# SwiGLU feed-forward on one core: the first half block of x by a crossbar copy instead of TensorE transposes, with a new order of loads and matmuls in the head

## Chip, core and metric

The kernel runs on one NeuronCore of one Trainium2 chip. The metric is the device time in microseconds (us) of that core. Three runs of the kernel before gave 163.2, 163.65 and 164.01 us, median 163.65 us.

## The reference

All tensors are bf16. B = 1, S = 2048 rows, D = 640, F = 1536.

```
g = silu(x @ w_gate)      # x [1, 2048, 640], w_gate [640, 1536]
u = x @ w_up              # w_up [640, 1536]
return (g * u) @ w_down   # w_down [1536, 640]
```

## The kernel before

The matmuls contract over the partitions, so x is needed transposed: `xT` holds 5 slices (`kd`) of 128 values of D on the partitions, and all 2048 rows of x along the free axis. S is cut into 4 blocks (`sb`) of 512 rows, F into 12 chunks (`fc`) of 128. For each block and chunk, five matmuls over `kd` make the gate `pg` and five make the up projection `pu`, both [128, 512] in PSUM; `gate` (L210) applies Silu on ScalarE and multiplies on VectorE, which writes the chunk to `aT`. After the 12 chunks of a block follow the down projection into `po_t` (the last 128 columns of D, transposed) and `po_a` (the first 512), and the output is sent off. VectorE also works out the last four rows of the output's hidden layer by dot products (`row_dots`), beside TensorE.

The part at issue is the start, `head` (L219). There the first block's first four chunks (`EARLY` = 4) are treated apart, since nothing has been loaded yet:

- TensorE runs 18 matmuls on a tile of ones (`warm`, L174), whose result is not used.
- Rows 0 to 255 of x are loaded as they lie (`load_x`, L85: one DMA of 128 rows on SyncE's queue, one on ScalarE's), and transposed by TensorE: `transpose_chunk` (L180), twice five transposes into PSUM, which ScalarE and VectorE copy to `xT`. This needs the identity matrix `ident`, made on GpSimd.
- Rows 256 to 511 are transposed on the way from memory by `turn_x` (L104), a crossbar copy (`dma_start_transpose`) on SyncE's queue. The later blocks' x comes in the same way.
- The order of the gate's matmuls is written out in `steps` (L230 to 235): for each `kd` the four chunks on rows 0 to 255, then for each `kd` the four chunks on rows 256 to 511; 44 matmuls in all. Then, chunk by chunk, the up projection on all 512 rows (20 matmuls of 512 columns) and the gate's Silu and product.

SyncE issues its DMAs in the order of the program (`keep_order`, L315). In the head it is: x rows 0 to 127, `w_gate` of the four early chunks in four DMAs by `kd` (the fifth, `kd` 1, on ScalarE's queue, L114), the crossbar copy of rows 256 to 511 (L118), `w_up` of the four early chunks in two DMAs (L121), then `w_gate` and `w_up` of chunks 4 to 7 and of chunks 8 to 11 (L123, L124), `w_down` (L125), and the crossbar copy of the second block's rows (L135). TensorE and ScalarE also run in the order of the program. The early loads are of these sizes: x rows 0 to 255 and 256 to 511, 320 KB each; `w_gate` and `w_up` of four chunks, 640 KB each.

Of the kernel before, what the change touches and what calls it, by code (L numbers as in the profile page):

```python
# [7 lines left out]


@with_exitstack  # L10
def _body(
# [8 lines left out]
    nc = tc.nc  # L20
    P = nc.NUM_PARTITIONS
    f32 = mybir.dt.float32
    bf16 = mybir.dt.bfloat16
# [3 lines left out]
    B, S0, D = x.shape  # L27
    F = w_gate.shape[1]
    S = B * S0
    x2 = x.rearrange("b s d -> (b s) d")  # L30
    out2 = out.rearrange("b s d -> (b s) d")

    KD = D // P
    KF = F // P
    S_BLK = 512
    NSB = S // S_BLK
    SUB = S_BLK // P
    HALF = S_BLK // 2
    DA = 512
    Q = 32  # L40
    N_WARM = 18
    T = 4
    WT_STEP = 4
    ROW_J = 0
    EARLY = 4
# [3 lines left out]
    consts = ctx.enter_context(tc.tile_pool(name="consts", bufs=1))  # L49
    work = ctx.enter_context(tc.tile_pool(name="work", bufs=3))  # L50
    outp = ctx.enter_context(tc.tile_pool(name="outp", bufs=3))
    psum = ctx.enter_context(
        tc.tile_pool(name="psum", bufs=2, space=bass.MemoryType.PSUM)
    )

    ident = consts.tile([P, P], bf16)
    x_sb = consts.tile([P, HALF // P, D], bf16)
    xT = consts.tile([P, KD, S], bf16)
    wg_sb = consts.tile([P, KD, F], bf16)
    wu_sb = consts.tile([P, KD, F], bf16)  # L60
# [7 lines left out]
    row_s = consts.tile([P, KF, T], f32)  # L68
    prod = consts.tile([P, D], f32)

    make_identity(nc, ident[:])

    x_v = x2.rearrange("(c p) d -> p c d", p=P)
    xt_v = x2.rearrange("s (kd p) -> s kd p", p=P)
    wg_v = w_gate.rearrange("(kd p) f -> p kd f", p=P)
    wu_v = w_up.rearrange("(kd p) f -> p kd f", p=P)
# [2 lines left out]
    def wslice(a, b):  # L79
        return slice(a * P, b * P)  # L80

    def load_w(eng, dst, src, a, b):
        eng.dma_start(out=dst[:, :, wslice(a, b)], in_=src[:, :, wslice(a, b)])

    def load_x(eng, c0, c1):  # L85
        eng.dma_start(out=x_sb[:, c0:c1, :], in_=x_v[:, c0:c1, :])  # L86

    def issue_order(a, b):
        tc.add_manual_dep(
# [8 lines left out]
    def keep_order(engine):  # L98

        traced = [i for i in nc.cur_bb.bb.instructions if i.engine == engine]  # L100
        for a, b in zip(traced, traced[1:]):
            issue_order(a, b)

    def turn_x(r0, r1):  # L104
        nc.sync.dma_start_transpose(out=xT[:, :, r0:r1], in_=xt_v[r0:r1])
# [2 lines left out]
    silu_first = consts.tile([P, 1], f32)  # L108
    nc.vector.memset(ones[:], 1.0)  # L109

    load_x(nc.sync, 0, 1)
    load_x(nc.scalar, 1, 2)
    for kd in range(KD):
        eng = nc.scalar if kd == 1 else nc.sync  # L114
        eng.dma_start(
            out=wg_sb[:, kd, wslice(0, EARLY)], in_=wg_v[:, kd, wslice(0, EARLY)]
        )
    turn_x(HALF, S_BLK)  # L118
    nc.scalar.activation(silu_first[:], ones[:, 0:1], ACT.Silu)  # L119
    for a in range(0, EARLY, 2):  # L120
        load_w(nc.sync, wu_sb, wu_v, a, a + 2)  # L121
    for a, b in W_CHUNKS:
        load_w(nc.sync, wg_sb, wg_v, a, b)  # L123
        load_w(nc.sync, wu_sb, wu_v, a, b)  # L124
# [4 lines left out]
    def turn_w(dst, src, f0, f1):  # L129
# [7 lines left out]
        out=x_row[:],  # L137
        in_=x2[S - T : S, :].rearrange("t d -> (t d)").partition_broadcast(P),
# [35 lines left out]
    def warm(n):  # L174
        for _ in range(n):
            nc.tensor.matmul(  # L176
                pw[:, 0:P], lhsT=ones[:], rhs=ones[:], start=True, stop=True
            )

    def transpose_chunk(c, parts):  # L180
        c_sl = slice(c * P, (c + 1) * P)
        for copy, tag, k0, k1 in parts:
            pt = psum.tile([P, k1 - k0, P], bf16, tag=tag, name="pt")
            for kd in range(k0, k1):
                nc.tensor.transpose(  # L185
                    out=pt[:, kd - k0, :],
                    in_=x_sb[:, c, kd * P : (kd + 1) * P],
                    identity=ident[:],
                )
            copy(out=xT[:, k0:k1, c_sl], in_=pt[:])  # L190

    def proj_step(ps, w_sb, fc, sb, c0, c1, kd):
        nc.tensor.matmul(  # L193
            ps[:, c0:c1],
            lhsT=w_sb[:, kd, fc * P : (fc + 1) * P],
            rhs=xT[:, kd, sb * S_BLK + c0 : sb * S_BLK + c1],
            start=(kd == 0 and c0 in (0, HALF)),
            stop=(kd == KD - 1),
        )

    def proj(ps, w_sb, fc, sb, c0, c1):
        for kd in range(KD):
            proj_step(ps, w_sb, fc, sb, c0, c1, kd)

    def gu_tiles():
        pg = psum.tile([P, S_BLK], f32, tag="gu", name="pg", bufs=4)
        pu = psum.tile([P, S_BLK], f32, tag="gu", name="pu", bufs=4)
        return pg, pu

    def gate(pg, pu, sb, fc, n_s):  # L210

        s0 = sb * S_BLK
        sg = work.tile([P, S_BLK], f32, name="sg")
        nc.scalar.activation(sg[:, 0:n_s], pg[:, 0:n_s], ACT.Silu)  # L214
        nc.vector.tensor_tensor(  # L215
            out=aT[:, fc, s0 : s0 + n_s], in0=sg[:, 0:n_s], in1=pu[:, 0:n_s], op=ALU.mult
        )

    def head():  # L219
        dve, act = nc.vector.tensor_copy, nc.scalar.copy  # L220
        split = [(act, "po_a", 0, 2), (dve, "po_b", 2, KD)]
        pgs = [
            psum.tile([P, S_BLK], f32, tag="gu", name="pg", bufs=4)
            for _ in range(EARLY)
        ]
        warm(N_WARM)
        for c in range(HALF // P):
            transpose_chunk(c, split)

        steps = [(0, 0, P), (0, P, HALF)]  # L230
        steps += [(kd, 0, HALF) for kd in range(1, KD)]
        steps += [(kd, HALF, S_BLK) for kd in range(KD)]
        for kd, c0, c1 in steps:
            for fc in range(EARLY):
                proj_step(pgs[fc], wg_sb, fc, 0, c0, c1, kd)

        for fc in range(EARLY):
            pu = psum.tile([P, S_BLK], f32, tag=("po_a", "po_b")[fc % 2], name="pu")
            proj(pu, wu_sb, fc, 0, 0, S_BLK)
            gate(pgs[fc], pu, 0, fc, S_BLK)  # L240
        keep_order(mybir.EngineType.PE)
        keep_order(mybir.EngineType.Activation)

    head()
    for sb in range(NSB):
        n_s = S_BLK if sb < NSB - 1 else S_BLK - T
        for fc in range(KF):
            if sb == 0 and fc < EARLY:
                continue
            pg, pu = gu_tiles()  # L250
# [22 lines left out]
        for q in range(P // Q):  # L273
            nc.scalar.dma_start(
                out=out2[
                    sb * S_BLK : sb * S_BLK + n_t, DA + q * Q : DA + (q + 1) * Q
                ].rearrange("(i r) c -> r i c", r=Q),
                in_=ot_q[q * Q : (q + 1) * Q, :].rearrange("r (i c) -> r i c", c=Q),
            )

        for j in range(SUB):
# [6 lines left out]
            for c0, c1, tag in cols:  # L288
# [14 lines left out]
                eng = nc.sync if c1 < D else nc.scalar  # L303
# [82 lines left out]
def kernel(tc, *args):  # L386
    _body(tc, *args)
    tc.close()
    tc.compile()
    _trim(tc.nc)  # L390
# [30 lines left out]
```

## Time and profile before

| | |
|---|---|
| three runs | 163.2, 163.65, 164.01 us |
| span of the profiled execution, first to last instruction | 161.8 us |
| time of the runs less that span | 1.4, 1.85 (median) and 2.2 us |
| granted TensorE clock, as the page has it | 1.00 |
| TensorE busy | 159.4 us, 99% of the span |
| VectorE, ScalarE, GpSimd busy | 111.0, 42.6, 0.6 us |
| read from memory, written to it | 6.88 MB, 2.62 MB |

The profiled execution's own time outside of its span isn't given; which of the three runs is nearest to it can't be told. "PE" is TensorE's matmuls, "PEld" its loads of weights, "DVE" VectorE, "ACT" ScalarE, "SPq" the issuing of DMAs by SyncE. A matmul's duration holds the time that it takes to drain, so the rate is read from how many begin in a stretch, not from the mean duration. In the list of DMA issues the last number is the time from issue to landing.

### The profile page before, as it was taken

The numbers are of one execution on the slowest core, as the hardware profiler recorded it, in microseconds if no ns is written. First come the engines' busy times: TensorE is split into PE (matmuls) and PEld (weight loads), VectorE is DVE, ScalarE is ACT, GpSimd is POOL, SyncE is SP. The second block draws the span as 40 slices with busy tenths as digits, with TensorE's granted clock in tenths as the row PEclk, the third lists the DMA queues.
The fourth block names the chain that finished last, engine by engine and source line by source line (L and its number), as shares of the span: only waits on it lengthen the run. The fifth ranks groups of instructions, "written<-read, shape, count | busy, mean of one in ns | idle before, by whom it ended". The sixth has DMA issues, their size and how long they took to land.

```text
span 161.8 us, 2142 instructions
## 1 busy us (share of the span) xinstructions
PE 159.4 (99%) x808; PEld 77.6 (48%) x808; DVE 111.0 (69%) x250; ACT 42.6 (26%) x74; POOL 0.6 (0%) x6
## 2 busy tenths in 40 slices
PE   8999999999999999999999999999999999999995
PEld 7854444444444444444444444444444444445454
DVE  2034223599569999989919999979964999993001
ACT  5051222112222222211222322221214222222121
POOL 1000000000000000000000000000000000000000
PEclk9999999999999999999999999999999999999999
DMA  6999999934189999003110000000321000000312
GB/s 212 231 351 349 361 248 231 222 75 91 34 192 159 235 236 184 4 0 34 65 65 0 0 4 2 0 0 3 62 67 34 0 0 0 0 0 4 48 41 73
DMA packets 41961, 15.86 MB, mean 98 GB/s; under 512 B 33504, under 2 KB 41824, under 8 KB 41952
## 3 DMA queue, kind: packets, MB, share of 16 engines
q1 hardware_dynamic: 33584, 14.93, 37.0%
q10 hardware_dynamic: 8368, 0.80, 3.5%
q8 instruction: 6, 0.10, 0.3%
q14 instruction: 3, 0.02, 0.1%
HBM read 6.88 MB, written 2.62 MB: 59 GB/s over the span
## 4 chain that ended last, share of the span: by engine, by line
PE 97%; DMA 2%; SPq 0%; DVE 0%; issue 0%
PE pg L193 32%; PE pu L193 32%; PE po_a L291 26%; PE po_t L261 6%; DMA wg_sb<-in_w_gate_dram 2%; SPq L86 0%; DVE ot_b L302 0%
## 5 line engine op out<-in xcount | busy, mean ns | idle before, releaser
L193 PE MATMUL pg<-xT,wg_sb 128*128 128x512 bf16 (+3 forms) x264 | 59.8, 363 | 0.1
L193 PE MATMUL pu<-xT,wu_sb 128*128 128x512 bf16 (+1 forms) x240 | 59.1, 379 | 0.0
L215 DVE TENSOR_TENSOR aT<-sg,pu 128x512 bf16<-128x512 f32 (+1 forms) x48 | 32.7, 682 | 32.3 <-PE pu L193 32.3
L214 ACT ACTIVATE sg<-pg 128x512 f32<-128x512 f32 (+1 forms) x48 | 28.4, 597 | 71.2 <-PE pg L193 67.4
L291 PE MATMUL po_a<-wd_sb,aT 128*128 128x512 bf16 (+4 forms) x228 | 42.8, 348 | 0.0
L147 DVE SCALAR_TENSOR_TENSOR prod<-wgT,x_row 128x640 f32<-128x640 bf16 x48 | 39.4, 821 | 1.5 <-DMA wgT<-in_w_gate_dram 0.4
L147 DVE SCALAR_TENSOR_TENSOR prod<-wuT,x_row 128x640 f32<-128x640 bf16 x48 | 39.4, 821 | 1.0
L193 PEld LDWEIGHTS <-wg_sb 128*128 128x128 bf16 x264 | 25.9, 100 | 26.8 <-DMA wg_sb<-in_w_gate_dram 0.4
L193 PEld LDWEIGHTS <-wu_sb 128*128 128x128 bf16 x240 | 23.4, 98 | 28.1 <-DMA wu_sb<-in_w_up_dram 0.3
L291 PEld LDWEIGHTS <-aT 128*128 128x128 bf16 x228 | 20.8, 98 | 21.7
L300 ACT CAST ot<-po_a 128x512 bf16<-128x512 f32 (+2 forms) x17 | 9.5, 559 | 31.8 <-PE po_a L291 20.2
L261 PE MATMUL po_t<-aT,wd_sb 128*128 128x512 bf16 (+1 forms) x48 | 10.4, 366 | 0.0
L261 PEld LDWEIGHTS <-wd_sb 128*128 128x128 bf16 x48 | 4.7, 98 | 5.1
L302 DVE CAST ot_b<-po_a 128x96 bf16<-128x96 f32 (+1 forms) x2 | 0.5, 240 | 9.7 <-PE po_a L291 9.6
L270 ACT CAST ot_t<-po_t 128x512 bf16<-128x512 f32 (+1 forms) x4 | 2.2, 559 | 11.6 <-PE po_t L261 11.6
L147 DVE DVE_READ_ACCUMULATOR prod<-wgT,x_row 128x1 f32 x48 | 3.9, 82 | 0.0
L147 DVE DVE_READ_ACCUMULATOR prod<-wuT,x_row 128x1 f32 x48 | 3.9, 82 | 0.0
L272 DVE STREAM_TRANSPOSE ot_q<-ot_t 128x512 bf16<-128x512 bf16 (+1 forms) x4 | 2.7, 676 | 1.7 <-ACT ot_t L270 1.7
L190 DVE COPY xT<-pt 128x384 bf16<-128x384 bf16 x2 | 0.7, 358 | 2.9 <-PE pt L185 2.9
L176 PE MATMUL pw<-ones 128*128 128x128 bf16 x18 | 2.1, 313 | 0.4 <-DVE ones L109 0.4
L176 PEld LDWEIGHTS <-ones 128*128 128x128 bf16 x18 | 1.8, 147 | 0.4 <-DVE ones L109 0.4
L119 ACT ACT_TABLE_LOAD x1 | 1.3, 1283 | 1.0 <-issue 1.0
(13 smaller groups left out, 4.7 us busy)
## 6 DMA issues: line engine op xcount, KB each, us to landing
wd_sb<-in_w_down_dram SPq DMA_DIRECT2D x1, 1920.0 KB, 13.0
out_dram<-ot SPq DMA_DIRECT2D x15, 128.0 KB, 1.7
wg_sb<-in_w_gate_dram SPq DMA_DIRECT2D x2, 640.0 KB, 7.9
wu_sb<-in_w_up_dram SPq DMA_DIRECT2D x2, 640.0 KB, 8.6
wu_sb<-in_w_up_dram SPq DMA_DIRECT2D x2, 320.0 KB, 4.7
x_row<-in_x_dram SPq DMA_DIRECT2D x1, 640.0 KB, 5.1
wg_sb<-in_w_gate_dram SPq DMA_DIRECT2D x4, 128.0 KB, 3.4
out_dram<-ot_q ACTq DMA_DIRECT2D x12, 32.0 KB, 1.9
```

Of the source, the lines that this page charges most:

```text
L119: nc.scalar.activation(silu_first[:], ones[:, 0:1], ACT.Silu)
L147: nc.vector.scalar_tensor_tensor(out=prod[:], in0=wT[:, fc, :], scalar=1.0, in1=x_row[:, t, :], op0=ALU.mult, op1=ALU.mult, accum_out=acc[ ...
L176: nc.tensor.matmul(pw[:, 0:P], lhsT=ones[:], rhs=ones[:], start=True, stop=True)
L190: copy(out=xT[:, k0:k1, c_sl], in_=pt[:])
L193: nc.tensor.matmul(ps[:, c0:c1], lhsT=w_sb[:, kd, fc * P : (fc + 1) * P], rhs=xT[:, kd, sb * S_BLK + c0 : sb * S_BLK + c1], start=(kd == 0 ...
L214: nc.scalar.activation(sg[:, 0:n_s], pg[:, 0:n_s], ACT.Silu)
L215: nc.vector.tensor_tensor(out=aT[:, fc, s0 : s0 + n_s], in0=sg[:, 0:n_s], in1=pu[:, 0:n_s], op=ALU.mult)
L261: nc.tensor.matmul(po_t[:], lhsT=wd_sb[:, kf, DA:D], rhs=aT[:, kf, sb * S_BLK : sb * S_BLK + n_t], start=(kf == 0), stop=(kf == KF - 1),)
L270: nc.scalar.copy(ot_t[:], po_t[:])
L272: nc.vector.transpose(out=ot_q[:], in_=ot_t[:])
L291: nc.tensor.matmul(po[:], lhsT=aT[:, kf, s0 : s0 + P], rhs=wd_sb[:, kf, c0:c1], start=(kf == 0), stop=(kf == KF - 1),)
L300: nc.scalar.copy(ot[:], po[:])
```

## The change

Rows 0 to 255 of x now come by `turn_x`, as the first DMA on SyncE's queue; `ident`, `x_sb`, the ten TensorE transposes and their four copies are gone. All loads of the head are on SyncE's queue; `w_gate` of the early chunks comes in three DMAs (`kd` 0; 1 and 2; 3 and 4). The crossbar copy of rows 256 to 511 is issued behind both DMAs of `w_up` instead of before them. There are 26 warming matmuls instead of 18. TensorE's order in the head is: gate of the four chunks on rows 0 to 255 (20 matmuls of 256 columns, `kd` outermost), up of the four chunks on rows 0 to 255 (20), gate of the four chunks on rows 256 to 511 (20), up on rows 256 to 511 (20), each of the last four groups of five followed by `gate`. The up projections take all four PSUM buffers of `po_a` and `po_b` at once. Behind the head nothing is changed.

```diff
-    N_WARM = 18
+    N_WARM = 26
...
-    ident = consts.tile([P, P], bf16)
-    x_sb = consts.tile([P, HALF // P, D], bf16)
...
-    make_identity(nc, ident[:])
...
-    load_x(nc.sync, 0, 1)
-    load_x(nc.scalar, 1, 2)
-    for kd in range(KD):
-        eng = nc.scalar if kd == 1 else nc.sync
+    def load_d(eng, k0, k1):
         eng.dma_start(
-            out=wg_sb[:, kd, wslice(0, EARLY)], in_=wg_v[:, kd, wslice(0, EARLY)]
+            out=wg_sb[:, k0:k1, wslice(0, EARLY)], in_=wg_v[:, k0:k1, wslice(0, EARLY)]
         )
-    turn_x(HALF, S_BLK)
+
     nc.scalar.activation(silu_first[:], ones[:, 0:1], ACT.Silu)
+    turn_x(0, HALF)
+    load_d(nc.sync, 0, 1)
+    load_d(nc.sync, 1, 3)
+    load_d(nc.sync, 3, KD)
     for a in range(0, EARLY, 2):
         load_w(nc.sync, wu_sb, wu_v, a, a + 2)
+    turn_x(HALF, S_BLK)
...
         warm(N_WARM)
-        for c in range(HALF // P):
-            transpose_chunk(c, split)
-
-        steps = [(0, 0, P), (0, P, HALF)]
-        steps += [(kd, 0, HALF) for kd in range(1, KD)]
-        steps += [(kd, HALF, S_BLK) for kd in range(KD)]
+        steps = [(kd, 0, HALF) for kd in range(KD)]
         for kd, c0, c1 in steps:
             for fc in range(EARLY):
                 proj_step(pgs[fc], wg_sb, fc, 0, c0, c1, kd)
-
+        pus = [
+            psum.tile([P, S_BLK], f32, tag=("po_a", "po_b")[fc % 2], name="pu")
+            for fc in range(EARLY)
+        ]
         for fc in range(EARLY):
-            pu = psum.tile([P, S_BLK], f32, tag=("po_a", "po_b")[fc % 2], name="pu")
-            proj(pu, wu_sb, fc, 0, 0, S_BLK)
-            gate(pgs[fc], pu, 0, fc, S_BLK)
+            proj(pus[fc], wu_sb, fc, 0, 0, HALF)
+
+        for fc in range(EARLY):
+            proj(pgs[fc], wg_sb, fc, 0, HALF, S_BLK)
+        for fc in range(EARLY):
+            proj(pus[fc], wu_sb, fc, 0, HALF, S_BLK)
+            gate(pgs[fc], pus[fc], 0, fc, S_BLK)
```

More of the change, by code (lines that the diff above doesn't have):

```diff
@@ L6 @@
 from concourse._compat import with_exitstack
-from concourse.masks import make_identity
 @with_exitstack
@@ L69, in _body @@
     prod = consts.tile([P, D], f32)
-    make_identity(nc, ident[:])
-    x_v = x2.rearrange("(c p) d -> p c d", p=P)
     xt_v = x2.rearrange("s (kd p) -> s kd p", p=P)
@@ L83, in load_w @@
         eng.dma_start(out=dst[:, :, wslice(a, b)], in_=src[:, :, wslice(a, b)])
-    def load_x(eng, c0, c1):
-        eng.dma_start(out=x_sb[:, c0:c1, :], in_=x_v[:, c0:c1, :])
     def issue_order(a, b):
@@ L178, in warm @@
             )
[L180 to L190, printed above, removed]
     def proj_step(ps, w_sb, fc, sb, c0, c1, kd):
@@ L219, in head @@
     def head():
-        dve, act = nc.vector.tensor_copy, nc.scalar.copy
-        split = [(act, "po_a", 0, 2), (dve, "po_b", 2, KD)]
         pgs = [
```

## The prediction

> **What bounds the kernel now.** First the page: busy times, and the chain that ended last.
>
> ```profile
> PE 159.4 (99%) x808; PEld 77.6 (48%) x808; DVE 111.0 (69%) x250; ACT 42.6 (26%) x74; POOL 0.6 (0%) x6
> ...
> PE 97%; DMA 2%; SPq 0%; DVE 0%; issue 0%
> ...
> L176 PE MATMUL pw<-ones 128*128 128x128 bf16 x18 | 2.1, 313 | 0.4 <-DVE ones L109 0.4
> ```
>
> TensorE carries the whole span, so the time is: the moment at which it begins useful work, plus that work, plus holes. The change leaves the work as it is and touches only the start, so the second view is the chain of the first 16 us.
>
> ```profile
> 0.45 3.21 DMA wg_sb<-in_w_gate_dram
> 3.66 0.05 issue
> 3.71 5.21 PE pg L193 x44
> 8.92 4.37 PE pu L193 x20
> 13.29 1.08 PE pg L193 x5
> ```
>
> From 3.71 us on TensorE is on the chain without a break. The head is over when the first ordinary group begins: 13.12 us in the timeline of TensorE (the chain counts ends and says 13.29). From there groups of five take 1.08 us each to the end. Whatever moves 13.12 moves the time by as much.
>
> ```profile
> 0.39 2.10 PE L176 MATMUL pw<-ones 128*128 128x128 bf16 x18 [0.39 <-DVE ones L109]
> 2.31 1.25 PE L185 MATMUL pt<-ident,x_sb 128*128 128x128 bf16 x10
> ...
> 13.12 1.24 PE L193 MATMUL pg<-xT,wg_sb 128*128 128x512 bf16 x5
> 14.20 1.03 PE L193 MATMUL pu<-xT,wu_sb 128*128 128x512 bf16 x4
> ```
>
> Third, the rate, from the stretches' counts of matmuls (one that began earlier is counted too).
>
> ```profile
> 3.71:4.95 1.24, 1.24 (x10) 1.00 1.01 265
> 4.97:6.48 1.51, 1.51 (x15) 1.00 0.86 185
> 6.57:8.75 2.18, 2.18 (x21) 1.00 0.97 291
> 8.79:13.12 4.33, 4.33 (x22) 1.00 1.07 353
> ```
>
> The 20 gate matmuls of 256 columns in 6.57 to 8.75 take 109 ns each, the 20 up matmuls of 512 columns 216 ns. The 18 warming matmuls of 128 columns, begun within 2.10 us less the last one's own 0.31 us (313 ns, the page's L176), stand 105 ns apart: as long as 256 columns take later. So the array begins at half speed, although the clock column says 1.00 throughout. In 3.71 to 4.95 us ten matmuls begin, eight of 128 and two of 256 columns, which would take 6 × 0.109 = 0.65 us at full speed; half speed costs the head 0.6 us now, and ends at about 5 us.
>
> Fourth, the loads: SyncE's issues (start, duration), then times to landing, each asked for in a stretch that holds that issue alone.
>
> ```profile
> 1.85 0.43 SPq L115 DMA_DIRECT2D wg_sb<-in_w_gate_dram  x1
> 2.33 1.91 SPq L105 DMA_TRANSPOSE xT<-in_x_dram  x1
> 4.29 1.15 SPq L83 DMA_DIRECT2D wu_sb<-in_w_up_dram  x2
> 5.49 0.52 SPq L83 DMA_DIRECT2D wg_sb<-in_w_gate_dram  x1
> 6.06 0.92 SPq L83 DMA_DIRECT2D wu_sb<-in_w_up_dram  x1
> ```
>
> ```profile
> x_sb<-in_x_dram ACTq DMA_DIRECT2D x1, 160.0 KB, 2.6
> wg_sb<-in_w_gate_dram SPq DMA_DIRECT2D x1, 128.0 KB, 3.4
> xT<-in_x_dram SPq DMA_TRANSPOSE x1, 4.2
> wu_sb<-in_w_up_dram SPq DMA_DIRECT2D x1, 320.0 KB, 4.9
> wg_sb<-in_w_gate_dram SPq DMA_DIRECT2D x1, 640.0 KB, 6.6
> wu_sb<-in_w_up_dram SPq DMA_DIRECT2D x1, 640.0 KB, 8.0
> ```
>
> With the issue times: x rows 0 to 255 are in at 2.7 us (ScalarE's DMA, issued at 0.13), the last early gate slice at 5.25, the crossbar copy at 2.33 + 4.2 = 6.5, the second early up load at 4.93 + 4.9 = 9.8, then gate 4 to 7 at 12.1 and up 4 to 7 at 14.0. TensorE wants the last at 14.2: only 0.2 us to spare. The loads therefore run close beside TensorE, and their order matters.
>
> **The change part by part.** *Removed:* identity, ten transposes, four copies. The transposes run from 2.31 to 3.3 us, in time in which TensorE otherwise waits for `w_gate` (ready at 3.66), so they free nothing. Two DMAs on ScalarE's queue go to SyncE; an issue takes some 0.4 us and SyncE stays ahead of the data. *Added:* 8 warming matmuls. 26 times 105 ns from 0.39 us end at 3.1 us; they delay nothing unless data come before that. *The work itself:* 80 matmuls of 256 columns at 109 ns, 8.72 us, against 40 × 109 + 20 × 216 = 8.68 us now. Nothing gained.
>
> *The price is in the arrivals.* Now the crossbar copy is hidden behind gate work on rows that came as plain loads. In the changed kernel everything waits for a crossbar copy, and the 40 matmuls on rows 256 to 511 (4.36 us) wait for a second one that stands behind 320 + 640 + 640 KB. Today the head's last data, at 9.8, leave 3.3 us of work behind them; there 4.36 us remain. To break even the second copy must land by 13.12 − 4.36 = 8.76 us.
>
> When does it land? First copy: bounded below by 2.7 us (the same 320 KB as plain loads at the start) and above by 4.2 (this copy behind the gate loads). Two copies of twice the size with a freer queue:
>
> ```profile
> 44.58 2.73 SPq L105 DMA_TRANSPOSE xT<-in_x_dram  x1
> ...
> xT<-in_x_dram SPq DMA_TRANSPOSE x1, 5.4
> ```
>
> ```profile
> 44.57:45.66 1.09, 1.09 (x7) 0.49 (x5) 0.00 (x0) 0.60 (x1) 0.00 (x0) 1.00 0.37 120
> 45.66:46.90 1.24, 1.24 (x7) 0.59 (x6) 1.13 (x2) 0.12 (x1) 0.00 (x0) 1.00 0.77 141
> 46.90:48.40 1.50, 1.50 (x9) 0.68 (x7) 1.47 (x5) 0.47 (x1) 0.00 (x0) 1.00 1.27 286
> ```
>
> The last column is GB/s. For 1.1 us only output stores move, then the copy runs at half rate for over a microsecond, then at 286 GB/s. A start of 1.1 us, 320 KB at these rates (175 KB in 1.24 us, the rest at 286 GB/s in 0.53) and 0.7 us from the last data to landing (today's copy, whose stretches stand below: data to about 5.8, landed at 6.5) give 3.6 us. I take 3.6, nearer to this row than to the plain loads. The Trainium skill ("Advanced Engine Details and Errata", X-Bar Transpose (TRN2)) says that transposing DMAs are as fast as regular ones, at 350 to 400 GB/s expected. The traced 286 GB/s after a stretch at 141 is below that. By the page the first copy would land with the plain loads, at 2.7.
>
> Behind a crossbar copy the queue has a hole. Here the stretches around today's landing at 6.5:
>
> ```profile
> 5.25:5.80 0.55, 0.00 (x0) 1.00 1.27 287
> 6.00:6.50 0.50, 0.00 (x0) 1.00 0.39 79
> 6.50:7.00 0.50, 0.00 (x0) 1.00 0.67 183
> 7.00:9.00 2.00, 0.00 (x0) 1.00 1.04 321
> ```
>
> So 640 KB behind a copy landed 9.8 − 6.5 = 3.3 us after it; the next 640 KB took 12.1 − 9.8 = 2.3 us; and a 320 KB copy landed 6.5 − 5.25 = 1.25 us behind the load ahead of it. By these landings: 3.6, gate 6.9, up 9.2, second copy 10.5 us. By bytes alone: after 3.6 the remaining 1.27 MB at 321 GB/s are 4.0 us, the slow ramp 0.3, the copy's 0.33 MB at 287 GB/s 1.1, landing 0.5: 9.5 us. The first counts how long the slowest of the DMA engines trails, the second doesn't; I take 10.1.
>
> First-half work: `kd` 0 lands some 0.9 us behind the copy, at 4.5 (an estimate from 128 of the 640 KB and the hole). Gate waits on the loads to 6.9, the last 8 of it end at 7.8, the 20 up matmuls wait for 9.2 at most and end at 10.3 by landings, sooner by bytes. So both ends meet near 10.1; then 4.36 us give 14.5 against 13.12: +1.35 us.
>
> *What is late next:* up 4 to 7. It landed 14.0 − 9.8 = 4.2 us behind the early up loads; behind a copy that is 3.3 + 2.3 = 5.6, at 15.7, and TensorE wants it at 14.5 + 1.08 = 15.6. I add 0.15 us. The loads for chunks 8 to 11 are wanted 8 groups or 8.6 us later, while their 1.31 MB take 4.1 us at 321 GB/s; the next crossbar copy is wanted by the second block, at least 16 groups or 17 us later. The new waits on PSUM are covered: the fifth gate group takes the buffer of the first, whose Silu can run as soon as its five matmuls on rows 256 to 511 are done, 3.8 us earlier. The fourth Silu waits for the first product's buffer, but its PSUM is wanted 3 us after the head.
>
> **Sum:** +1.35 + 0.15 = +1.5 us on the span of 161.8; with the 1.85 us by which the median exceeds that span, 163.65 + 1.5 = 165.15 us.
>
> **Rivals.** *A: the copy is as quick as a plain load and the loads keep their rate.* First copy at 2.7, second by bytes 5.9 us later, at 8.6, below the 8.76 of the break-even. Then TensorE itself is the bound: from `kd` 0 at 3.5 us with 8.72 us of work and some 0.7 us lost to half speed, the head ends at 12.9: −0.2 us, 163.45, not slower. For it speaks the 287 GB/s that a copy reaches; against it the first microsecond without data and the hole, which both stand in rows. It decides from a second landing before 8.8; in between lie times within 0.5%.
>
> *B: the array stays at half speed.* Between the warming's end at 3.1 and `kd` 0 at 4.5 TensorE is idle for 1.4 us, against 0.4 today, and then it waits between the gate slices. If full speed isn't granted through all of the first half, 40 matmuls at 210 ns (twice the 105) from 4.5 end at 12.9, not at 10.1: 2.8 us more, 167.95 us. For it: half speed is seen until about 5 us today, with TensorE busy nearly throughout. Against: full speed came in spite of a hole of 0.4 us. The Trainium skill ("TensorE: Matmul & The Clock Gate", Part 1) puts the release after about 3.4 us of sustained work, judged in windows that run freely. One window later would, by that figure as an estimate, release at about 8.4 us and cost only some 0.5 us, because the first half waits for loads anyway.
>
> *C: up 4 to 7 ends last.* If it trails further, the head's end no longer decides: each 0.1 us past 15.6 adds as much. Up to 0.5 us, 165.65; it is inside the range.
>
> **How the numbers follow.** A measurement of this kernel can tell about 0.5%, 0.8 us, from no change. Forecast (with C) 0.70, from +0.8 us on; A and its neighbours 0.20, of which 0.17 within 0.5%; B 0.10. The first copy between 2.7 and 4.2 is −0.9 to +0.6 us on the 3.6, the second by bytes or by landings −0.6 to +0.4, C up to +0.5: from 0.0 to +3.0 us with all low or all high ends together. All ends at once are rare, so I cut both a little, to +0.15 and +2.75 us: 163.8 to 166.4, with A's gain and most of B outside. Slower by over 0.5%: 0.80; within: 0.17; faster: 0.03, since even without a wait the head can't be 0.8 us shorter than now unless full speed comes earlier too.
>
> **What would show it.** Right: the chain begins with the crossbar copy and `w_gate`, the first gate matmul starts at 4 to 5 us, the gate on rows 256 to 511 waits for `xT` at about 10, the first ordinary group starts at 14 to 15, and from there groups last 1.08 us. Wrong, towards A: `xT` in by 3 us, no wait for the second copy. Towards B: 256-column matmuls 210 ns apart beyond 6 us. Any difference behind the head would be against all of it.

## The result, and the profile after

The changed kernel takes 165.38 us (median of 6 runs, 164.22 to 166.14) against 163.64 us, a ratio of 1.0104 with a 95% interval of 1.0071 to 1.0137: 1.7 us slower, where 1.5 us were forecast. One of the six executions of the kernel before took 165.71 us, over 1.5% above the fastest, and counts as slow. The profiled execution of the changed kernel is the fastest of its six, 164.22 us with a span of 162.9: 1.1 us longer than the span before. In all executions listed with their spans the time is 1.26 to 1.39 us above the span, so the trace before, with 161.8 us, fits its fastest execution too (163.2), and not the median. The page says of the changed kernel:

```profile
PE 158.2 (97%) x811; PEld 78.7 (48%) x822; DVE 110.1 (68%) x248; ACT 42.0 (26%) x72; POOL 0.2 (0%) x4
```

TensorE now leaves 3% of the span idle instead of 1%. The chain of that execution's start tells where:

```profile
2.02 3.73 DMA wg_sb<-in_w_gate_dram
5.74 0.05 issue
5.79 1.92 PE pg L174 x16
7.71 2.19 PE pu L174 x20
9.89 2.31 PE pg L174 x20
```

The chain runs back to `w_gate`, not to the second crossbar copy. The timeline of TensorE in the same trace (start, duration from the first start to the last end, count, idle time before) and one of its stretches (length, busy time of TensorE with the count of matmuls, granted clock, DMA share, GB/s):

```profile
5.08 2.63 PE L174 MATMUL pg<-xT,wg_sb 128*128 128x256 bf16 x20 [1.72 <-DMA wg_sb<-in_w_gate_dram]
...
7.55 2.35 PE L174 MATMUL pu<-xT,wu_sb 128*128 128x256 bf16 x20
...
9.86 2.34 PE L174 MATMUL pg<-xT,wg_sb 128*128 128x256 bf16 x20
...
14.22 1.24 PE L174 MATMUL pg<-xT,wg_sb 128*128 128x512 bf16 x4
```

```profile
5.79:7.50 1.71, 1.71 (x16) 1.00 1.04 312
```

The first gate matmul begins at 5.08 us (3.71 before). The 16 behind the wait for the second slice stand 107 ns apart: full speed, where the kernel before lost 0.6 us to half speed. The first ordinary group begins at 14.22 us, before at 13.12. The start at 5.08, work of 8.72 us and 0.4 us of holes make up 14.2. Against the kernel before that is +1.4 us of start, −0.6 of half speed and +0.3 of other waits and pace: 1.1 us, the whole difference of the spans.

The issues (start, duration) and times to landing of the same trace, each from a stretch with one issue:

```profile
1.40 0.56 SPq L103 DMA_DIRECT2D wg_sb<-in_w_gate_dram  x1
2.48 0.47 SPq L103 DMA_DIRECT2D wg_sb<-in_w_gate_dram  x1
3.51 0.53 SPq L77 DMA_DIRECT2D wu_sb<-in_w_up_dram  x1
4.08 3.02 SPq L96 DMA_TRANSPOSE xT<-in_x_dram  x1
7.77 0.57 SPq L77 DMA_DIRECT2D wu_sb<-in_w_up_dram  x1
```

```profile
xT<-in_x_dram SPq DMA_TRANSPOSE x1, 3.5
wg_sb<-in_w_gate_dram SPq DMA_DIRECT2D x1, 128.0 KB, 3.6
wg_sb<-in_w_gate_dram SPq DMA_DIRECT2D x1, 256.0 KB, 4.0
wu_sb<-in_w_up_dram SPq DMA_DIRECT2D x1, 320.0 KB, 5.1
xT<-in_x_dram SPq DMA_TRANSPOSE x1, 5.7
wu_sb<-in_w_up_dram SPq DMA_DIRECT2D x1, 640.0 KB, 6.5
```

So the first copy is in at 3.5 us (forecast 3.6), gate slice 0 at 5.0 (4.5), the last gate slices at 6.5 (6.9), the early up loads at 8.6 (9.2), the second copy at 9.8 (10.1), up 4 to 7 at 14.3 (15.7). The hole behind the first copy stands in the rates:

```profile
1.25:2.75 1.50, 0.00 (x0) 1.00 0.99 208
2.75:3.50 0.75, 0.00 (x0) 1.00 0.69 161
3.50:4.25 0.75, 0.00 (x0) 1.00 0.84 221
```

For the first 1.3 us no data move at all; by the bytes moved, most of the copy's 320 KB are through at about 2.75 us. Until 4.25 the loads behind it run at 161 and 221 GB/s, where the next 0.75 us have 341.

This execution explains 1.1 us, the medians differ by 1.7. The rest is in the other executions. Of twelve executions of the changed kernel (these six and six of a repetition, below), four took 164.2 to 164.6 us and eight 165.2 to 166.1, with nothing in between. One execution of each group has a trace.

### The profile page after: what moved, and what is told of

Read it like the earlier page. It is cut to its first block, busy times and chain, and to the rows that moved or that the text cites. A ratio compares the mean times of both kernels' runs of the same rounds, so it can differ in the third digit from the quotient of the medians.

```text
span 162.9 us, 2147 instructions
## 1 busy us (share of the span) xinstructions
PE 158.2 (97%) x811; PEld 78.7 (48%) x822; DVE 110.1 (68%) x248; ACT 42.0 (26%) x72; POOL 0.2 (0%) x4
## 4 chain that ended last, share of the span: by engine, by line
PE 95%; DMA 2%; SPq 1%; issue 0%; DVE 0%
PE pu L174 32%; PE pg L174 31%; PE po_a L272 26%; PE po_t L242 6%; DMA wg_sb<-in_w_gate_dram 2%; SPq L96 1%; SPq L103 0%; DVE ot_b L283 0%
## 5 line engine op out<-in xcount | busy, mean ns | idle before, releaser
L174 PE MATMUL pg<-xT,wg_sb 128*128 128x512 bf16 (+2 forms) x253 | 59.1, 362 | 2.2 <-DMA wg_sb<-in_w_gate_dram 1.7
L174 PE MATMUL pu<-xT,wu_sb 128*128 128x512 bf16 (+2 forms) x260 | 59.3, 362 | 0.0
L272 PE MATMUL po_a<-wd_sb,aT 128*128 128x512 bf16 (+4 forms) x224 | 42.3, 348 | 0.2
L174 PEld LDWEIGHTS <-wg_sb 128*128 128x128 bf16 x260 | 25.3, 98 | 28.6 <-DMA wg_sb<-in_w_gate_dram 2.4
L174 PEld LDWEIGHTS <-wu_sb 128*128 128x128 bf16 x260 | 25.3, 98 | 26.4
L169 PE MATMUL pw<-ones 128*128 128x128 bf16 x26 | 3.0, 313 | 0.4 <-DVE ones L100 0.4
L169 PEld LDWEIGHTS <-ones 128*128 128x128 bf16 x26 | 2.7, 148 | 0.4 <-DVE ones L100 0.4
```

The source lines that it names most:

```text
L169: nc.tensor.matmul(pw[:, 0:P], lhsT=ones[:], rhs=ones[:], start=True, stop=True)
L174: nc.tensor.matmul(ps[:, c0:c1], lhsT=w_sb[:, kd, fc * P : (fc + 1) * P], rhs=xT[:, kd, sb * S_BLK + c0 : sb * S_BLK + c1], start=(kd == 0 ...
L272: nc.tensor.matmul(po[:], lhsT=aT[:, kf, s0 : s0 + P], rhs=wd_sb[:, kf, c0:c1], start=(kf == 0), stop=(kf == KF - 1),)
```

## The experiments

Three theories were to be told apart. *Arrivals at the end*, the prediction's own: the second copy sets the end of the head. *Arrivals at the start*: the first gate slice, late behind the first copy, sets it. *Half speed* (the "clock theory" of the expectations): the idle stretch between warming and first gate matmul (3.2 to 5.1 us) keeps the array at half speed in many executions. Ratios are to the kernel before, run beside each experiment.

**e8: the changed kernel again** (no edit).

> The changed kernel unaltered, with 26 warming matmuls, beside e5 on the same chip and for a second trace: 165.4 us. Clock theory: a trace that isn't the fastest of its runs shows the first gate matmuls at half speed, 213 ns apart for 256 columns, for part of the first half; arrival theory: the loads land later in it instead.

Measured: 165.56 us against 163.31 beside it, ratio 1.0112 (1.0078 to 1.0146; the medians alone would give 1.0138, with two of the six among the short executions). The profiled execution is one of the long ones, 165.82 us. Its chain and stretches:

```profile
4.77 4.45 PE pg L174 x20
9.22 2.41 PE pu L174 x20
11.63 2.18 PE pg L174 x20
13.81 2.18 PE pu L174 x20
```

```profile
4.77:9.60 4.83, 4.83 (x23) 1.00 1.16 282
11.46:15.82 4.36, 4.36 (x42) 1.00 1.10 349
```

The loads land slightly sooner than in the other trace (first gate matmul at 4.77 instead of 5.08), and still the head ends 1.6 us later, at 15.83. In 4.77 to 9.60 us 23 matmuls of 256 columns take 210 ns each; the 40 in 11.46 to 15.82, at 109, half as much (42 counted, with those that began before). The clock column says 1.00 all along. From 4.77 TensorE has no hole at all: no matmul waits for a load, nor for the second copy. That speaks for half speed, and against later loads, as the cause of this long execution; that the other seven long ones have the same cause is inferred from their times. It is the sign that the prediction had named for its rival B: 210 ns beyond 6 us.

**e1: 44 warming matmuls** (`N_WARM = 26` becomes 44; TensorE is then busy until 4.7 us).

> 44 warming matmuls in place of 26, so that TensorE is busy from 0.4 us until the first gate slice lands at about 5 us (44 x 0.106 = 4.7 us). Arrival theory: nothing changes, the loads set the start and the second copy the end of the wait; same as the changed kernel, 165.4 us median, about 1% over the kernel before. Clock theory (the changed kernel's median is 1.2 us above its profiled execution because in other executions the array is still at half speed behind the idle stretch from 3.2 to 5 us): median falls by 0.5 to 1 us to about 164.6, and the executions lie closer together. If warming reaches past the landing, it can cost up to 0.2 us.

Measured: 164.49 us (163.98 to 165.09, 12 runs), ratio 1.0045 (1.0028 to 1.0062), 0.9 us under the changed kernel, and none of the twelve above 165.1. The trace:

```profile
3.83 0.78 PE L169 MATMUL pw<-ones 128*128 128x128 bf16 x11
4.74 0.61 PE L174 MATMUL pg<-xT,wg_sb 128*128 128x256 bf16 x4
5.64 1.92 PE L174 MATMUL pg<-xT,wg_sb 128*128 128x256 bf16 x16 [0.28 <-DMA wg_sb<-in_w_gate_dram]
...
14.04 1.24 PE L174 MATMUL pg<-xT,wg_sb 128*128 128x512 bf16 x5
```

Full speed comes within the warming itself: 33 of the 44 begin by 3.8 us, 104 ns apart, and the last 11 follow about twice as fast. So the gate matmuls are at full speed (16 in 1.92 us), TensorE waits for gate slice 1 until 5.64, and the head ends at 14.04. For the second copy it doesn't wait: the up projection ends at 7.48 + 20 × 0.109 = 9.66 and the gate goes on at 9.67. Nothing was changed in the loads, so about half of the 1.7 us, 0.9, belongs to half speed. What is left, 0.85 us by the medians and 0.75 by the ratio (0.45%), is the late start with the waits for gate slices behind it, less the 0.6 us of half speed that the trace of the kernel before has and this one hasn't.

**e5: 18 warming matmuls** (`N_WARM = 26` becomes 18).

> The changed kernel with 18 warming matmuls instead of 26 (TensorE idle from 2.3 us, not 3.2, until the first gate slice at about 5). Arrival theory alone: no change against the changed kernel (165.4). Clock theory: the longer idle stretch makes the half-speed start outlast the loads more often, 0.5 to 1.5 us more: 166 to 167, and a trace with 256-column matmuls 213 ns apart beyond 6 us.

Measured: 165.62 us (165.31 to 166.7, 5 runs), ratio 1.015 (1.0119 to 1.0182). The median is that of the repetition beside it, 165.56, not the 166 to 167 expected; but none of the five is below 165.3. The trace has the half speed:

```profile
4.65:8.80 4.15, 4.15 (x20) 1.00 1.19 243
```

Twenty matmuls at 208 ns until 8.8 us. In this trace the longer idle stretch doesn't lengthen the half speed (8.8 us against 9.6 in the repetition); with five runs it can't be said whether it makes it more frequent.

**e2: gate slice 0 ahead of the copy.**

```diff
-    turn_x(0, HALF)
     load_d(nc.sync, 0, 1)
+    turn_x(0, HALF)
```

> The first gate slice (128 KB) is issued ahead of the first crossbar copy instead of behind it. Hole theory (a load behind a crossbar copy lands 1.5 us after it): the slice lands at about 2.5 us, the copy some 0.4 us later than now, at 3.9 to 4.1; the first gate matmul starts at 4.0 instead of 5.1, but the next slices still come through the hole, at about 5.8. If the second copy's landing (9.8 us, same bytes ahead of it) sets the end of the head, the head ends where it does now, 14.2 us, and the time stays within 0.2 us of the changed kernel. If the start sets it, up to 0.7 us are won.

Measured: 167.37 us, ratio 1.0225 (1.0201 to 1.0249), 2 us above the changed kernel, which neither theory of the expectation had. Slice 0 does land early, at 2.2 us, and the copy at 4.2, so four gate matmuls start at 4.26. But then slices 1 and 2 come through the hole at 6.4 us and TensorE idles again:

```profile
4.26:5.00 0.74, 0.74 (x4) 1.00 0.94 233
6.40:11.28 4.88, 4.88 (x24) 1.00 1.15 279
11.42:12.70 1.28, 1.28 (x14) 1.00 1.10 357
```

24 matmuls take 203 ns each until 11.3 us. Half speed lasts longest in this trace, the one with two idle stretches, and all six executions are above 167 us.

**e6: the same with 52 warming matmuls** (busy until 5.5 us).

> The first gate slice ahead of the copy, as in e2, but with 52 warming matmuls (busy until about 5.9 us), so that the array is at full speed when the loads come. Clock theory: the 3.7 us that e2 lost against the kernel before fall to about 1: the second copy lands at 10.2 as in e2, 4.36 us of work follow, the head ends at 14.6, the time is 164.5 to 165. If it stays near 167, e2's loss was not the clock.

Measured: 165.21 us, ratio 1.0104 (1.0083 to 1.0125): 1.2% less than without the warming, as expected of half speed, though a little above the 164.5 to 165 forecast. In the trace:

```profile
6.78 1.92 PE L174 MATMUL pg<-xT,wg_sb 128*128 128x256 bf16 x16 [0.70 <-DMA wg_sb<-in_w_gate_dram]
...
15.12 1.24 PE L174 MATMUL pg<-xT,wg_sb 128*128 128x512 bf16 x4
```

It is at full speed from 6.78 on, and the head ends at 15.1, not 14.6, because the slices behind the copy come so late: 6.78 and 76 matmuls at 0.109 make 15.06. Here too it isn't the second copy that is waited for.

**e3: gate slices on the other queue.**

```diff
     turn_x(0, HALF)
-    load_d(nc.sync, 0, 1)
-    load_d(nc.sync, 1, 3)
-    load_d(nc.sync, 3, KD)
+    load_d(nc.scalar, 0, 1)
+    load_d(nc.scalar, 1, 3)
+    load_d(nc.scalar, 3, KD)
```

(The first Silu is issued behind them.)

> The three DMAs of the early gate slices go to the other hardware queue (ScalarE's), issued at once beside the first crossbar copy. If the hole behind a copy belongs to its queue (the next packets wait for the copy's landing), the slices land from about 2.5 to 4.5 us and the copy later, at 4 to 4.5, by shared bandwidth; the gate starts at 4 to 4.5 instead of 5.1, the second copy lands some 0.5 to 1 us sooner than 9.8, and the time falls by 0.5 to 0.8 us against the changed kernel. If the copy holds up the DMA engines themselves, the slices land at 5 us as now and nothing is won.

Measured: 165.93 us, ratio 1.013 (1.0106 to 1.0155), not faster, where 0.5 to 0.8 us less were expected. The two lists of issues and TensorE's timeline:

```profile
wg_sb<-in_w_gate_dram ACTq DMA_DIRECT2D x1, 128.0 KB, 2.7
xT<-in_x_dram SPq DMA_TRANSPOSE x1, 5.5
```

```profile
5.57 3.70 PE L174 MATMUL pg<-xT,wg_sb 128*128 128x256 bf16 x20 [2.23 <-DMA xT<-in_x_dram]
...
15.66 1.24 PE L174 MATMUL pg<-xT,wg_sb 128*128 128x512 bf16 x5
```

Slice 0 lands at 2.8 us, so on a queue of its own it doesn't wait behind the copy, as the first theory had it; but the copy itself now takes 5.5 us instead of 3.5, and TensorE waits for x. The first 20 matmuls (3.70 us) are partly at half speed again.

**e7: the second copy back in its place** (crossbar copy first, but the second copy behind the gate slices, TensorE's order of the kernel before, 44 warming matmuls).

```diff
     load_d(nc.sync, 3, KD)
+    turn_x(HALF, S_BLK)
...
-    turn_x(HALF, S_BLK)
...
-        steps = [(kd, 0, HALF) for kd in range(KD)]
+        steps = [(kd, 0, HALF) for kd in range(KD)]
+        steps += [(kd, HALF, S_BLK) for kd in range(KD)]
```

> The crossbar copy first, but the second copy and TensorE's order as in the kernel before (copy behind the gate slices, gate on all 512 rows, then up on all 512), with 44 warming matmuls. If the second copy's place is what costs, it lands at about 7.6 instead of 9.6 and the time falls below that of e1 (164.5) towards 163.9. If the late start costs, the early up loads are then late (about 9.8 and 10.8) and the head ends at 14.1 again: 164.5, the same as e1.

Measured: 164.32 us, ratio 1.0059 (1.0038 to 1.008), the interval overlaps with that of the 44 warming matmuls alone, 1.0028 to 1.0062. The copy's issue and its time to landing, then the chain and TensorE's timeline:

```profile
2.99 2.14 SPq L96 DMA_TRANSPOSE xT<-in_x_dram  x1
...
xT<-in_x_dram SPq DMA_TRANSPOSE x1, 4.6
```

```profile
2.99 4.61 DMA xT<-in_x_dram
7.61 0.04 issue
7.65 2.34 PE pg L174 x20
...
10.04 4.26 PE L174 MATMUL pu<-xT,wu_sb 128*128 128x512 bf16 x19
14.15 1.24 PE L174 MATMUL pg<-xT,wg_sb 128*128 128x512 bf16 x5
```

The second copy lands two us sooner, at 7.6, and the head still ends at 14.15 (14.04). The sooner copy isn't free of waits either: in this order the gate wants it sooner, and TensorE waits for it until 7.65, some 0.4 us (5.06, the first gate matmul, and 20 × 0.109 make 7.24). So the place of the second copy, moved together with the order that goes with it, makes no difference that can be measured.

**e4: the order alone** (x rows 0 to 255 by plain loads and TensorE's transposes, 18 warming matmuls, as before; copy behind `w_up` and TensorE's order as in the changed kernel).

```diff
-    turn_x(HALF, S_BLK)
     nc.scalar.activation(silu_first[:], ones[:, 0:1], ACT.Silu)
     for a in range(0, EARLY, 2):
         load_w(nc.sync, wu_sb, wu_v, a, a + 2)
+    turn_x(HALF, S_BLK)
```

> One part of the change alone: rows 0 to 255 again as plain loads with TensorE's transposes and 18 warming matmuls as in the kernel before; the second part is kept (rows 256 to 511 copied behind w_up, up on rows 0 to 255 first). Arrival theory: the first gate matmul starts at 3.7 as before, the first half needs 5 us to about 8.7, the copy lands at about 9.0, so the head ends at 13.3 to 13.5: 0.2 to 0.4 us over the kernel before, and 0.8 to 1.4 under the changed kernel. If the new order were the cost, the time would be that of the changed kernel.

Measured: 163.72 us (12 runs), ratio 1.0007 (0.9988 to 1.0026): no measurable difference to the kernel before. Its trace is of one of its three longest executions, 164.41 us, and shows a wait for the up load:

```profile
7.80 2.36 PE L193 MATMUL pu<-xT,wu_sb 128*128 128x256 bf16 x20 [0.98 <-DMA wu_sb<-in_w_up_dram]
...
14.39 1.24 PE L193 MATMUL pg<-xT,wg_sb 128*128 128x512 bf16 x5
```

So in the median the order costs and gains nothing, though it can bring a wait. What the change costs comes with the crossbar copy as the first DMA, together with what was changed beside it: the gate slices in three DMAs behind it on the same queue, and 26 warming matmuls that end 1.6 to 1.9 us too early.

**e9: the kernel before with one warming matmul** (`warm(N_WARM)` becomes `warm(1)`), to see half speed without a crossbar copy at the start.

> The kernel before with one warming matmul in place of 18: TensorE idle from 0.5 us to the first transpose at 2.3, all loads as they are. Arrival theory alone: no change, 163.6. Clock theory: the array stays at half speed for longer, as in the changed kernel's slower executions, although there is no crossbar copy at the start: 0.5 to 2 us more, 164 to 165.5, with 256-column matmuls 213 ns apart in the trace beyond 5 us.

Measured: 164.52 us (163.59 to 164.88, 10 runs), ratio 1.0046 (1.0027 to 1.0065). The trace:

```profile
4.50:8.29 3.79, 3.79 (x20) 1.00 0.82 194
8.30:9.93 1.63, 1.63 (x17) 1.00 1.12 348
```

Until 8.3 us the matmuls stand twice as far apart as behind it. Idle time ahead of the first useful matmul costs 0.9 us by the medians here too (0.75 by the ratio), without any change of a load.

**e10: slice 0 beside x in the kernel before** (gate slices 0 and 2 on ScalarE's queue, both x loads on SyncE's), an attempt at an earlier start.

> The kernel before with gate slices 0 and 2 on ScalarE's queue and both x loads on SyncE's, so that the first slice runs beside the first 128 rows of x instead of behind them: it lands at about 2.5 us instead of 3.66, the second x load at about 3.1 instead of 2.7, and the first gate matmul starts at 3.3 to 3.5 instead of 3.71. If the start sets the head's end, 0.1 to 0.3 us less than the kernel before (163.3 to 163.5), at most 0.2%, since the extra work is done at half speed; if the later loads set it, no change.

Measured: 163.84 us, ratio 1.0014 (1.0002 to 1.0027): slightly slower and not faster. Its chain waits for the second x load; below it, from the timeline, the gate:

```profile
0.46 2.99 DMA x_sb<-in_x_dram
3.45 0.05 issue
3.49 0.71 PE pt L186 x5
...
4.00 6.00 PE L194 MATMUL pg<-xT,wg_sb 128*128 128x128 bf16 x44
```

What the slice wins the second half of x loses: the gate starts at 4.00 us, not at 3.71. In this trace, of the longest of the twelve executions, that is the smaller part. Its 44 gate matmuls take 6.00 us against 5.21, because half speed lasts longer: in 5.20 to 7.00 us 11 matmuls are counted, in the kernel before 18. No idle stretch before them is longer than 0.2 us, so a late release of full speed isn't bound to a long gap. No version tried beats the kernel before.

## Why the prediction came out as it did

The time was foreseen within 0.25 us, and the sign. That the time came so close is luck: two of the reasons held, but the wait that carried most of the sum was hardly there, and a rival given 0.10 made up about half of the loss.

- *Everything before the head's end counts in full*: held. The spans differ by the shift of the first ordinary group, 1.1 us in the first trace; behind the head nothing moved (from the first ordinary group to the end it is 148.7 us in both traces, and in the trace of the repetition).
- *The first copy at 3.6 us*: held, 3.5. The prediction quoted the Trainium skill ("Advanced Engine Details and Errata", X-Bar Transpose (TRN2)) for copies as fast as plain loads. The trace disagrees for 320 KB: 3.5 against 2.7 us. The prediction had gone by the rows and not by the page.
- *Gate slice 0 some 0.9 us behind the copy*: too short. It was 1.5 us in the first trace and 1.2 in the second, and this term turned out to be the one that starts TensorE.
- *"To break even the second copy must land by 13.12 − 4.36 = 8.76 us"*, with the second copy as the last wait: this step failed as the cause. The copy did land close to the forecast (9.8, not 10.1), but TensorE waited for it only 0.13 us in the first trace (7.55 + 20 × 0.109 = 9.73, next start 9.86) and not at all in the second. The prediction had noted that both ends meet; it then took the copy's. With 44 warming matmuls TensorE doesn't wait for the second copy either, and the order without the crossbar copy at the start costs nothing in the median (1.0007). What sets the end is the start, the waits for gate slices and the work.
- *Up 4 to 7 too late, +0.15 us (C)*: wrong. It landed at 14.3 and was wanted at 15.3.
- *Half speed (B, 10%)*: much too low. By the times it is in eight of twelve executions (one of them traced), though in that trace for 23 matmuls and not all 40: 23 × 0.1 = 2.3 us, of which 0.4 replace waits for loads and 0.3 an earlier start, so 1.6 us at the head's end. In the kernel before, with TensorE nearly always busy from 0.4 us, it cost 0.6. The Trainium skill ("TensorE: Matmul & The Clock Gate", Part 1) has the release decided in windows of about 3.4 us that run freely, so that it falls differently in each execution. The traces agree with a release that comes late behind idle time and not at the same moment: full speed from 5.8 us at the latest in one trace of the same kernel, from 9.6 in another. With warming up to the loads it came between 3.9 and 5.1 us (three traces). The prediction's estimate from that page, 0.5 us for a release one window later, was too small: the release came at 9.6 and not at 8.4, and the waits for loads, which were to take up most of the loss, were only 0.4 us.

So the 1.7 us are, about half each, late start (0.75 to 0.85, what is left with 44 warming matmuls) and half speed (0.9 to 0.95, what these take away). The forecast put 1.35 into the wait for the second copy and 0.15 into the load behind it: near in sum, wrong in its parts. That idle time ahead of the first useful matmul prolongs the half speed is shown by the warming matmuls, which alter no load: more of them take 0.9 us away in the changed kernel, and nearly all of them left out adds 0.9 to the kernel before. How much idle time is too much, and which moment decides in an execution, stays open.

## What to carry to other kernels

The transfer that replaced work of a waiting engine saved nothing here; what counted was when the first operands of the bounding engine were complete, and the crossbar copy at the head of the queue delayed also what stood behind it. When the first useful matmul moves, let the warming matmuls reach up to it: the gap of 1.6 to 1.9 us cost about as much as the late loads themselves. And one trace is one execution: here the fastest one hid a third of the loss, and only the list of all executions, with its gap between 164.6 and 165.2, gave it away.

## What the runs showed of the hardware

- The granted clock is given as 1.00 in stretches in which 256-column matmuls begin 203 to 210 ns apart, against 109 later. The rate has to be counted.
- Full speed begins between 3.9 and 5.1 us in the three traces with 44 or 52 warming matmuls from 0.4 us on without a break, and only at 8.3 to 11.3 us in five traces with idle stretches of 0.9 to 2.2 us ahead of the first useful matmuls. In a sixth such trace (1.7 us idle), the fastest execution of the changed kernel, it is there by 5.8 us; and in one with no idle stretch over 0.2 us it comes only at about 7.2.
- A 320 KB crossbar copy as the first DMA moves no data for 1.3 us, is mostly through at 2.75 and lands at 3.5; the next 128 KB land 1.2 to 1.5 us behind it. With 640 KB of loads on another queue beside it the same copy lands at 5.5 us.
- A load issued first, ahead of that copy on the same queue, lands at 2.2 us, and the copy at 4.2.
